# Retention attention and routed experts on one core: key-value states moved ahead, more load buffers, x stored for two chunks at a time

## The chip, the cores and the metric

The kernel runs on one core of one Trainium2 chip. A core has a matrix engine (TensorE, PE in the profile), VectorE (DVE), ScalarE (ACT), GpSimd (POOL) and SyncE (SP), which here only issues transfers, and 16 DMA engines[...]. The metric is device time in microseconds for one execution, lower is better; the number before is the median of three runs.

## What is computed

The first half is a retention layer on (8, 8, 576, 64) tensors (batch, heads, positions, head size), the second a mixture of eight experts with one expert for each token. Between them, x is the attention output with its heads side by side, 4608 tokens of 512 features.

```python
scores = scale * q @ k.T;  ret = scores * Dmat        # Dmat[i, j] = gamma[head] ** (i - j) for i >= j, else 0
x = (ret @ v), heads side by side                     # (8, 576, 512)
logits = x @ w_gate                                   # 8 experts
local_gate = sigmoid(x @ w_local)
e = argmax(logits) if s == 0 or local_gate < 0.5 else the expert of the token before
out[b, s] = softmax(logits)[e] * (relu(x[b, s] @ w1[e]) @ w2[e])
```

## The kernel before

The 4608 tokens are cut into NCH = 36 chunks of 128. A batch has 576 positions, so PER = 9 chunks hold two batches, and the middle one (MID, m = 4) belongs half to each. Retention is computed in chunks: inside a chunk by scores that are masked and multiplied with the values, and between chunks by a key-value state. The decay is folded into q (`decq`) and v (`deck`), so a state is a plain running sum of k times v in PSUM.

For chunk i there are four functions, and a loop at the end of the first part calls them skewed: in round i, `scores(i + 1)`, `outputs(i)`, `rows(i - 1)`, `logits(i - 2)`.

- `scores(i)` loads one tile `ld` (1 MB: q and k by feature, k and v by token; line 156, on SP's queue), scales q into `qT` (VectorE, line 165) and v into `vs` (GpSimd, line 169), multiplies k and q into two PSUM tiles `sps` (TensorE, line 176, eight matmuls) and masks them into `sT` (VectorE, line 180). For even i from 4 on it also issues, behind its own load, a 256 KB piece of the first expert's weights (line 162).
- `outputs(i)` multiplies `vs` with `sT` into the PSUM tile `ops` (line 202), adds the state of the chunk before times `qT` (line 211), adds this chunk's k times v to the PSUM tile `kv` (line 221) and copies that to one of two `states` tiles (ScalarE, line 224). Then ScalarE copies `ops` to `xT` (line 226).
- `rows(i)` computes gates and logits in parts from `xT` (line 234, ScalarE copies `parts`, line 237), turns `xT` into `x` with a VectorE transpose of 32 by 32 blocks (line 242) and stores x to DRAM (`xd`) in four transfers of 64 KB, issued by ScalarE (line 244).
- `logits(i)` adds the parts up (`lps`, line 254); after each of five groups of chunks the routing (`route`) goes on in small steps on VectorE, GpSimd and TensorE.

TensorE's order is the program order (a manual schedule); the other engines' order comes from the framework's scheduler. [...] Pools decide how many buffers a tile has: five for `ld`, four for `qT` and `vs`, three for `sT`, `xT` and `x`, one for `ops` and one for `kv`. A load of `ld` can't start before the last reader of its buffer is done. That reader is usually the state matmul, which reads the keys by token:

```python
nc.tensor.matmul(kv[r, c, :], lhsT=kn[k, h], rhs=vs[k, h], ...)      # kn = ld[:, 2]
```

Every transfer on SP's or ACT's queue counts on one of eight semaphores (DMAHW0 to DMAHW7 in the built program), which the framework deals out in turn. A transfer that reuses a semaphore waits until the transfer that last had it has landed; an engine that issues it stands still until then.

The second part comes when routing is done: the tokens of each expert are gathered from `xd` and taken through both weight matrices in blocks (lines 655 to 714). A first, small block with 256 tokens known early fills TensorE while the last routing steps run, from about 201 to 243 us.

Of the kernel before, what the change touches and what calls it, by code (L numbers as in the profile page):

```python
# [12 lines left out]
F32 = mybir.dt.float32  # L13
# [9 lines left out]
P = 128  # L23
# [3 lines left out]
DK, FK = D // P, F // P  # L27
HP = H // 2
NTOK = B * S
NCH = NTOK // P  # L30
PER = 2 * S // P
# [24 lines left out]
GW = E + 2  # L56
SQ = 32
NSQ = P // SQ
assert NSQ == DK


@with_exitstack
def kernel(
# [10 lines left out]
    nc = tc.nc  # L74

    def pool(stack, name, bufs, space=None):
        kw = {} if space is None else {"space": space}
        return stack.enter_context(tc.tile_pool(name=name, bufs=bufs, **kw))
# [6 lines left out]
    xd = dram.tile([NTOK, D], F32, name="xd")  # L85
# [32 lines left out]

    with ExitStack() as part:
        once = pool(part, "once", 1)  # L120
        raw = pool(part, "raw", 5)
        work = pool(part, "work", 3)
        ps_s = pool(part, "ps_s", 2, PSUM)
        ps_o = pool(part, "ps_o", 1, PSUM)
# [13 lines left out]
            out=mask, in_=mask, compare_op=Alu.is_ge, fill=0.0,  # L138
            base=0, pattern=[[1, P]], channel_multiplier=-1)
        states = [once.tile([P, HP, DH], F32, name=f"state{i}") for i in range(2)]  # L140
        chunks = [{} for _ in range(NCH)]
        to_lanes, routing = [], []
        kv = None

        def scores(i):
            m = i % PER
            g = chunks[i]
            ld = raw.tile([P, 4, D], F32, name="ld")
            if i == MID:
                nc.sync.dma_start(out=decq[:, m].rearrange("p c t -> p (c t)"), in_=dq[:, 1])  # L150
            elif 0 < i < PER:
                for c in range(HP):
                    nc.scalar.activation(decq[:, m, c], decq[:, 0, c], Act.Copy, scale=later_q[:, m, c:c + 1])
            cut = 4 if i == 0 else 1
            for k in range(0, 4, 4 // cut):
                loaded = nc.sync.dma_start(out=ld[:, k:k + 4 // cut].rearrange("p t x -> p (t x)"),
                                           in_=qkv[i][:, k * D:(k + 4 // cut) * D])
            if 4 <= i < 4 + 4 * FK and i % 2 == 0:

                k, t = divmod(i // 2 - 2, 2)  # L160
                with tc.issue_after(loaded.ins):
                    nc.sync.dma_start(out=(w2s[0][:, k] if t else w1s[0][:, k].rearrange("p k f -> p (k f)")),
                                      in_=(w2 if t else w1)[0][:, k * D:(k + 1) * D])
            qT = work.tile([P, HP, P], F32, name="qT", bufs=4)
            nc.vector.tensor_tensor(qT, ld[:, 0].rearrange("p (c s) -> p c s", c=HP), decq[:, m], op=Alu.mult)  # L165
            kT = ld[:, 1].rearrange("p (c s) -> p c s", c=HP)
            kn, vn = ld[:, 2], ld[:, 3]
            vs = work.tile([P, D], F32, name="vs", bufs=4)
            scaled = nc.gpsimd.tensor_tensor(  # L169
                vs.rearrange("p (h d) -> p h d", h=H), vn.rearrange("p (h d) -> p h d", h=H),  # L170
                deck[:, m, :].unsqueeze(2).to_broadcast([P, H, DH]), op=Alu.mult)
            sps = [ps_s.tile([P, HP, P], F32, name=f"sps{u}", tag="s") for u in range(2)]
            for c in range(HP):
                for u in range(2):
                    r = slice(u * DH, (u + 1) * DH)
                    nc.tensor.matmul(sps[u][:, c, :], lhsT=kT[r, c, :], rhs=qT[r, c, :],  # L176
                                     start=True, stop=True, skip_group_check=True)
            sT = work.tile([P, 2, HP, P], F32, name="sT")
            for u in range(2):
                nc.vector.tensor_tensor(  # L180
                    sT[:, u], sps[u],
                    (mask2 if m == MID else mask).unsqueeze(1).to_broadcast([P, HP, P]), op=Alu.mult)
            g.update(qT=qT, kn=kn, vs=vs, sT=sT)

            with tc.issue_after(scaled.ins):
                for write in to_lanes[:2]:
                    write()
            del to_lanes[:2]

        def outputs(i):  # L190
            nonlocal kv
            m = i % PER
            g = chunks[i]
            qT, kn, vs, sT = g["qT"], g["kn"], g["vs"], g["sT"]


            ops = ps_o.tile([P, 2, HP, P], F32, name="ops")
            for c in range(HP):
                for u in range(2):
                    r = slice((u ^ c & 1) * DH, ((u ^ c & 1) + 1) * DH)  # L200
                    h = 2 * c + u
                    nc.tensor.matmul(ops[r, c & 1, c // 2, :], lhsT=vs[:, h * DH:(h + 1) * DH], rhs=sT[:, u, c, :],  # L202
                                     start=(c < 2), stop=(m == 0), skip_group_check=True)
            if m > 0:

                n = HALF if m == MID else P
                for c in range(HP):
                    for u in range(2):
                        k = slice(u * DH, (u + 1) * DH)
                        r = slice((u ^ c & 1) * DH, ((u ^ c & 1) + 1) * DH)  # L210
                        nc.tensor.matmul(ops[r, c & 1, c // 2, 0:n], lhsT=states[(i + 1) % 2][k, c, :],
                                         rhs=qT[k, c, 0:n], start=False, stop=True, skip_group_check=True)
            if m != PER - 1:
                k = slice(HALF, P) if m == MID else slice(0, P)
                if m in (0, MID):
                    kv = ps_kv.tile([P, HP, DH], F32, name="kv")
                for c in range(HP):
                    for u in range(2):
                        r = slice(u * DH, (u + 1) * DH)
                        h = slice((2 * c + u) * DH, (2 * c + u + 1) * DH)  # L220
                        nc.tensor.matmul(kv[r, c, :], lhsT=kn[k, h], rhs=vs[k, h],
                                         start=(m in (0, MID) and c == 0), stop=True,
                                         skip_group_check=True)
                nc.scalar.copy(states[i % 2], kv)
            g["xT"] = xT = work.tile([P, HP, P], F32, name="xT")
            nc.scalar.copy(xT.rearrange("p (a b) t -> p b a t", b=2), ops[:, :, 0:HP // 2])  # L226

        def rows(i):
            nonlocal lt, lps
            xT = chunks[i]["xT"]  # L230

            gps = ps_g.tile([P, P], F32, name="gps")
            for c in range(DK):
                nc.tensor.matmul(gps[c * SQ:(c + 1) * SQ, :], lhsT=gates[:, c, :], rhs=xT[:, c, :],
                                 start=True, stop=True, skip_group_check=True)
            parts = work.tile([P, P], F32, name="parts")
            nc.scalar.copy(parts, gps)
            chunks[i]["parts"] = parts


            x = work.tile([P, NSQ, DK, SQ], F32, name="x")
            nc.vector.transpose(x.rearrange("p t c r -> p t c r"), xT.rearrange("p c (t s) -> p t c s", s=SQ))  # L242
            for a in range(NSQ):
                nc.scalar.dma_start(
                    out=xd[i * P:(i + 1) * P, a * P:(a + 1) * P].rearrange("(t s) d -> s t d", s=SQ),
                    in_=x[a * SQ:(a + 1) * SQ].rearrange("p t c r -> p t (c r)"))

        def logits(i):

# [141 lines left out]
        with tc.manual_schedule(engines={ET.PE}):  # L391
            scores(0)
            scores(1)
# [7 lines left out]
        def number(name, shape, pattern, base=0, channel=0, dtype=F32):  # L401
# [13 lines left out]
            out=before, in_=before, compare_op=Alu.is_gt, fill=0.0,  # L415
# [14 lines left out]
        low = table.tile([P, P], F32, name="low")  # L430
        nc.vector.memset(low, -1.0)
        last_e = low[:, 0:1]
        lt = lps = None

        add_parts = once.tile([P, GW], F32, name="add_parts")
        for c in range(DK):
# [3 lines left out]
        for M, at in ((P // 2, 0), (P // 4, 0), (P // 4, P // 2)):  # L440
            r = repeat[M, at] = table.tile([P, P], F32, name=f"repeat{M}_{at}")
# [13 lines left out]
        with tc.manual_schedule(engines={ET.PE}):  # L455
            for i in range(NCH + 2):
                if 1 < i + 1 < NCH:
                    scores(i + 1)
                if i < NCH:
                    outputs(i)  # L460
                if 0 <= i - 1 < NCH:
                    rows(i - 1)
                if 0 <= i - 2:
                    logits(i - 2)
                    for step in routing:
                        next(step, None)
                    if i - 2 in ends[:-1]:
                        k = ends.index(i - 2)
                        routing.append(route(starts[k], GROUPS[k], lt))
                if i == ends[SOON - 1] + 5:  # L470
                    base_soon = base
                if i == ends[SOON - 1] + 5 + -(-GROUPS[SOON - 1] // 2):
                    routing.append(load_soon())
# [368 lines left out]
```

## Time and profile before

| | |
|---|---|
| time, median of 3 | 786.47 us (783.32 to 786.67) |
| span of the profiled execution | 788.9 us |
| TensorE busy | 715.0 us (91%) |
| VectorE, ScalarE, GpSimd busy | 155.7, 157.3, 250.6 us |
| loads of `ld` | 35 of 1024 KB and 4 of 256 KB, 7.0 and 5.7 us from issue to landing (median) |
| stores of x | 144 of 64 KB, 5.1 us to landing |
| mean granted TensorE clock | 0.96 |

How to read it: a busy share is a mean over stages. The page's 40 slices show that VectorE works almost only in the first ten or eleven slices (to about 237 us), where attention and routing run. The DMA engines are mostly 0.6 to 0.9 busy for the first nine slices and then work in bursts. TensorE is busy in 0.9 or more of most slices after that. "Granted clock" is the share of full speed that the chip gave to TensorE in a stretch.

### The profile page before, as it was taken

The page shows a single profiled execution, that of the slowest core. Times are in us where ns is not written, and L with a number is a line of the kernel's source. Part 1 is how long each engine was busy: PE and PEld are TensorE (multiplying, and loading weights), DVE is VectorE, ACT ScalarE, POOL GpSimd, SP SyncE. Part 2 cuts the span into 40 slices and gives each one's busy share as a digit, 9 for nine tenths or more (in the row PEclk, how much of TensorE's full clock was granted, in tenths as well). Part 3 has the DMA queues.
Part 4 walks back from the last instruction along what each step waited for, and adds up shares of the span by engine and source line. Part 5 has one row for each costly group of instructions (what it writes and reads, how often), then busy time and mean ns, then how long its engine had stood idle before and what let it go on. Part 6 is the DMA issues. An engine that isn't in the chain of part 4 may idle for free. (4 is left out here: it accounts for less than half of the span.)

```text
span 788.9 us, 12435 instructions
## 1 busy us (share of the span) xinstructions
PE 715.0 (91%) x4932; PEld 475.6 (60%) x4932; DVE 155.7 (20%) x448; ACT 157.3 (20%) x396; POOL 250.6 (32%) x343
## 2 busy tenths in 40 slices
PE   3998789899769999998999999999999989989991
PEld 3767677677654546745764674576468457547740
DVE  5655656667770000000000000000000000000000
ACT  5312122122202102202211220211122021112110
POOL 4132525342757017006201700630170071025003
PEclk9998799998789999999999999999999999999997
DMA  8689788894007006104500710350071053013001
GB/s 338 212 289 315 243 287 278 278 301 121 25 0 247 17 30 254 49 2 147 200 1 30 275 47 2 109 232 1 23 268 66 2 183 141 1 57 117 2 16 62
DMA packets 46535, 103.90 MB, mean 132 GB/s; under 512 B 8264, under 2 KB 26828, under 8 KB 41936
## 3 DMA queue, kind: packets, MB, share of 16 engines
q0 software_dynamic: 17184, 50.36, 17.4%
q1 hardware_dynamic: 8064, 42.21, 15.3%
q10 hardware_dynamic: 21168, 9.83, 4.5%
q8 instruction: 64, 1.05, 0.6%
q14 instruction: 55, 0.45, 0.2%
HBM read 90.82 MB, written 24.12 MB: 146 GB/s over the span
## 5 line engine op out<-in xcount | busy, mean ns | idle before, releaser
L712 PE MATMUL hps<-xT,w1s 128*128 128x304 f32 (+4 forms) x1024 | 259.1, 415 | 0.1
L655 PE MATMUL yps<-w2s,hT 128*128 128x512 f32 x528 | 237.2, 597 | 0.3 <-issue 0.3
L712 PEld LDWEIGHTS hps<-xT,w1s 128*128 128x128 f32 x1024 | 195.6, 191 | 63.7 <-issue 13.7
L634 POOL DMA_INDIRECT out_dram<-ys,rows x49 | 48.7, 995 | 362.2 <-ACT ys L659 349.8
L655 PEld LDWEIGHTS yps<-w2s,hT 128*128 128x128 f32 x528 | 96.9, 191 | 106.3 <-issue 105.9
L714 ACT ACTIVATE hT<-hps 128x304 f32<-128x304 f32 (+4 forms) x128 | 53.5, 418 | 218.1 <-PE hps L712 218.1
L751 DVE MEMSET rows<- 128x1 int32 (+1 forms) x27 | 1.4, 60 | 443.2 <-DMA out_dram<-ys,rows 426.4
L169 POOL TENSOR_TENSOR vs<-ld,decs 128x512 f32<-128x512 f32 x36 | 47.1, 1309 | 100.3 <-DMA ld<-in_qkv_dram 80.6
L176 PE MATMUL sps<-qT,ld 64*128 64x128 f32 x576 | 54.6, 316 | 22.7 <-DVE sT L180 8.7
L623 POOL DMA_INDIRECT xg<-xd,slot x54 | 54.9, 1018 | 21.4 <-issue 12.2
L176 PEld LDWEIGHTS sps<-qT,ld 64*128 64x128 f32 x576 | 44.9, 213 | 27.7 <-DVE sT L180 12.9
L202 PE MATMUL ops<-sT,vs 128*64 128x128 f32 x576 | 46.3, 309 | 8.7 <-ACT xT L226 3.9
L659 ACT ACTIVATE ys<-yps,slot 128x512 f32<-128x512 f32 x31 | 21.3, 687 | 155.9 <-PE yps L655 155.9
L180 DVE TENSOR_TENSOR sT<-sps,mask 128x512 f32<-128x512 f32 x72 | 46.3, 677 | 11.5 <-PE sps L176 11.4
L202 PEld LDWEIGHTS ops<-sT,vs 128*64 128x64 f32 x576 | 36.5, 154 | 14.2 <-issue 9.8
L697 PEld LDWEIGHTS hps<-ident,xg 128*128 128x128 f32 (+3 forms) x164 | 19.9, 147 | 39.4 <-ACT xT L698 22.8
L226 ACT COPY xT<-ops 128x512 f32<-128x512 f32 x36 | 21.1, 587 | 110.2 <-DMA xd<-x 30.8
L697 PE MATMUL hps<-ident,xg 128*128 128x128 f32 (+3 forms) x164 | 25.2, 281 | 14.7 <-ACT xT L698 13.2
L165 DVE TENSOR_TENSOR qT<-ld,decq 128x512 f32<-128x512 f32 x36 | 27.2, 759 | 41.8 <-DMA ld<-in_qkv_dram 37.4
L682 PE MATMUL yps<-w2s,hT 128*32 128x128 f32 (+1 forms) x544 | 30.1, 306 | 0.0
L242 DVE STREAM_TRANSPOSE x<-xT 128x512 f32<-128x512 f32 x36 | 25.4, 706 | 17.7 <-ACT xT L226 16.9
L682 PEld LDWEIGHTS yps<-w2s,hT 128*32 128x32 f32 (+1 forms) x544 | 21.2, 118 | 5.2
(192 smaller groups left out, 406.0 us busy)
## 6 DMA issues: line engine op xcount, KB each, us to landing
ld<-in_qkv_dram SPq DMA_DIRECT2D x35, 1024.0 KB, 7.0
w1s<-in_w_dram POOLq DMA_DIRECT2D x32, 512.0 KB, 8.7
w2s<-in_w_dram POOLq DMA_DIRECT2D x32, 512.0 KB, 5.6
xd<-x ACTq DMA_DIRECT2D x144, 64.0 KB, 5.1
w1s<-in_w_dram SPq DMA_DIRECT2D x8, 256.0 KB, 5.6
w2s<-in_w_dram SPq DMA_DIRECT2D x8, 256.0 KB, 5.6
ld<-in_qkv_dram SPq DMA_DIRECT2D x4, 256.0 KB, 5.7
xg<-xd,slot POOLq DMA_INDIRECT x54, 6.2
```

The costliest lines, as they stand in the source:

```text
L165: nc.vector.tensor_tensor(qT, ld[:, 0].rearrange("p (c s) -> p c s", c=HP), decq[:, m], op=Alu.mult)
L169: scaled = nc.gpsimd.tensor_tensor(vs.rearrange("p (h d) -> p h d", h=H), vn.rearrange("p (h d) -> p h d", h=H), deck[:, m, :].unsqueeze(2 ...
L176: nc.tensor.matmul(sps[u][:, c, :], lhsT=kT[r, c, :], rhs=qT[r, c, :], start=True, stop=True, skip_group_check=True)
L180: nc.vector.tensor_tensor(sT[:, u], sps[u], (mask2 if m == MID else mask).unsqueeze(1).to_broadcast([P, HP, P]), op=Alu.mult)
L202: nc.tensor.matmul(ops[r, c & 1, c // 2, :], lhsT=vs[:, h * DH:(h + 1) * DH], rhs=sT[:, u, c, :], start=(c < 2), stop=(m == 0), skip_group ...
L623: nc.gpsimd.indirect_dma_start(out=xgs[j % 2][:, g, :], out_offset=None, in_=xd, in_offset=bass.IndirectOffsetOnAxis(ap=slot[:, g, 0:1], a ...
L634: nc.gpsimd.indirect_dma_start(out=next(views).rearrange("t (q d) -> (t q) d", q=n), out_offset=bass.IndirectOffsetOnAxis(ap=rows, axis=0) ...
L655: nc.tensor.matmul(yps, lhsT=hT[:, m, g * P:(g + 1) * P], rhs=w[:, m, :], start=(m == 0), stop=(m == FK - 1))
L682: nc.tensor.matmul(yps[q * M:(q + 1) * M, 0:D // n], lhsT=hT[:, m, first:first + M], rhs=w[:, m, q * D // n:(q + 1) * D // n], start=(m == ...
L697: nc.tensor.transpose(xps[:, c, 0:M], xg[0:M, g, c * P:(c + 1) * P], ident[0:M, 0:M])
L712: nc.tensor.matmul(hps[:, 0:T // n], lhsT=w[:, m, c, :], rhs=xT[:, c, cols], start=(c == 0), stop=(c == DK - 1))
L714: nc.scalar.activation(hT[:, m, cols], hps[:, 0:T // n], Act.Relu)
```

## The change

Three things are changed, all in the first part.

- The state work is taken out of `outputs` into a function `state(i)`, called right after `outputs(i - 1)`, so that it runs one round sooner; in round 0 `state(0)` and `state(1)` both run. It is meant to let go of the load buffer sooner, and to have the state ready well before its reader.
- `ld` gets seven buffers instead of five. The room comes from `sT` and `xT`, which go from three to two.
- x of two chunks lies in one tile (two such tiles, instead of three for one chunk each), and after the odd chunk four transfers of 128 KB store both, where there were eight of 64 KB. It halves the number of issues on ScalarE and of turns on the eight semaphores.

```diff
-        raw = pool(part, "raw", 5)
+        raw = pool(part, "raw", 7)
...
-            sT = work.tile([P, 2, HP, P], F32, name="sT")
+            sT = work.tile([P, 2, HP, P], F32, name="sT", bufs=2)
...
+            g["xT"] = xT = work.tile([P, HP, P], F32, name="xT", bufs=2)
+            nc.scalar.copy(xT.rearrange("p (a b) t -> p b a t", b=2), ops[:, :, 0:HP // 2])
+
+        def state(i):
+            nonlocal kv
+            m = i % PER
+            kn, vs = chunks[i]["kn"], chunks[i]["vs"]
             if m != PER - 1:
                 k = slice(HALF, P) if m == MID else slice(0, P)
...
                 nc.scalar.copy(states[i % 2], kv)
-            g["xT"] = xT = work.tile([P, HP, P], F32, name="xT")
-            nc.scalar.copy(xT.rearrange("p (a b) t -> p b a t", b=2), ops[:, :, 0:HP // 2])
...
-            x = work.tile([P, NSQ, DK, SQ], F32, name="x")
-            nc.vector.transpose(x.rearrange("p t c r -> p t c r"), xT.rearrange("p c (t s) -> p t c s", s=SQ))
-            for a in range(NSQ):
-                nc.scalar.dma_start(
-                    out=xd[i * P:(i + 1) * P, a * P:(a + 1) * P].rearrange("(t s) d -> s t d", s=SQ),
-                    in_=x[a * SQ:(a + 1) * SQ].rearrange("p t c r -> p t (c r)"))
+            if i % 2 == 0:
+                x = work.tile([P, 2, NSQ, DK, SQ], F32, name="x", bufs=2)
+            nc.vector.transpose(x[:, i % 2], xT.rearrange("p c (t s) -> p t c s", s=SQ))
+            if i % 2:
+                for a in range(NSQ):
+                    nc.scalar.dma_start(
+                        out=xd[(i - 1) * P:(i + 1) * P, a * P:(a + 1) * P].rearrange("(t s) d -> s t d", s=SQ),
+                        in_=x[a * SQ:(a + 1) * SQ].rearrange("p b t c r -> p (b t) (c r)"))
...
                     outputs(i)
+                    for k in (0, 1) if i == 0 else (i + 1,):
+                        if k < NCH:
+                            state(k)
```

More of the change, by code (lines that the diff above doesn't have):

```diff
@@ L58 @@
 NSQ = P // SQ
-assert NSQ == DK
+assert NSQ == DK and NCH % 2 == 0
 @with_exitstack
@@ L190, in outputs @@
         def outputs(i):
-            nonlocal kv
             m = i % PER
             g = chunks[i]
-            qT, kn, vs, sT = g["qT"], g["kn"], g["vs"], g["sT"]
+            qT, vs, sT = g["qT"], g["vs"], g["sT"]
             ops = ps_o.tile([P, 2, HP, P], F32, name="ops")
@@ L224, in outputs @@
                 nc.scalar.copy(states[i % 2], kv)
-            g["xT"] = xT = work.tile([P, HP, P], F32, name="xT")
-            nc.scalar.copy(xT.rearrange("p (a b) t -> p b a t", b=2), ops[:, :, 0:HP // 2])
         def rows(i):
-            nonlocal lt, lps
+            nonlocal x
             xT = chunks[i]["xT"]
@@ L432 @@
         last_e = low[:, 0:1]
-        lt = lps = None
+        lt = lps = x = None
         add_parts = once.tile([P, GW], F32, name="add_parts")
```

## The prediction

> **What bounds the kernel now.** I read the page first: TensorE busy for 91% of the span, the chain that ended last too short to help, VectorE busy in the first ten of the 40 slices only. So the kernel has two parts: attention with routing, to about 200 us, and the expert blocks, in which TensorE hardly stops. The change touches the first part alone, so I went on to the windows of ten microseconds (TensorE, its weight loads, VectorE, ScalarE, GpSimd, then granted clock, DMA share, GB/s).
>
> ```profile
> 10.00:20.00 10.00, 5.59 (x48) 4.55 (x48) 7.48 (x15) 3.77 (x12) 7.38 (x31) 1.00 1.01 407
> 20.00:30.00 10.00, 8.88 (x120) 7.36 (x120) 6.05 (x10) 3.96 (x12) 1.31 (x2) 1.00 0.39 116
> 60.00:70.00 10.00, 7.68 (x91) 6.34 (x90) 5.91 (x15) 1.16 (x4) 2.98 (x2) 0.71 0.99 332
> 80.00:90.00 10.00, 6.04 (x103) 5.02 (x104) 5.62 (x19) 2.06 (x6) 3.11 (x7) 0.91 0.86 278
> 90.00:100.00 10.00, 10.00 (x126) 8.17 (x129) 5.78 (x13) 1.79 (x4) 6.49 (x11) 0.58 0.60 186
> 0.00:180.00 180.00, 147.83 (x2317) 119.41 (x2317) 109.45 (x254) 45.59 (x126) 68.59 (x113) 0.93 0.84 282
> ```
>
> To see there: the DMA engines are full from 10 to 20, nearly idle from 20 to 30 (five load buffers are full, none is free), and 0.84 busy over 180 us: 151 us of work, 29 us of idling. A window with TensorE idle (60, 80) is followed by a low clock (0.71, 0.58). Next, the DMA queue's own waits (total, times, longest):
>
> ```profile
> SPq L156 <- DMA xd<-x: 52.0, 12, 8.3
> SPq L156 <- PE kv L221: 49.0, 14, 8.0
> SPq L162 <- DMA xd<-x: 22.4, 9, 3.8
> ```
>
> A load is held half the time by its buffer (the key-value matmul that reads `kn` last) and half by a store of x. The built instruction order shows why a load waits for a store: SP and ACT share eight DMA semaphores, DMAHW0 to 7, and a DMA waits until the one that last used its semaphore has landed. Stores take four turns for a chunk, a load one, a weight piece half of one. Then the timeline, once where loads are late and once where ScalarE is held:
>
> ```profile
> 62.48 0.69 DVE L165 TENSOR_TENSOR qT<-ld,decq 128x512 f32<-128x512 f32 x1 [3.85 <-DMA ld<-in_qkv_dram]
> ...
> 63.72 1.25 DVE L180 TENSOR_TENSOR sT<-sps,mask 128x512 f32<-128x512 f32 x2
> ...
> 64.43 0.79 PE L176 MATMUL sps<-qT,ld 64*128 64x128 f32 x2 [2.32 <-DVE sT L180]
> ```
>
> ```profile
> 106.61 4.19 ACTq L244 DMA_DIRECT2D xd<-x  x4
> 110.84 0.59 ACT L226 COPY xT<-ops 128x512 f32<-128x512 f32 x1 [5.73 <-DMA xd<-x]
> ...
> 111.57 1.03 PE L202 MATMUL ops<-sT,vs 128*64 128x128 f32 x11 [2.43 <-ACT xT L226]
> ```
>
> In the first, `qT` of a chunk two ahead stands before `sT` on VectorE, so a late load stops the scores. In the second, four stores wait for semaphores 4.19 us, `xT` stands behind them, and `ops` has one buffer, so TensorE stops. Last, the end of the stage: the last load's consumer and the last attention matmul.
>
> ```profile
> 181.84 1.04 POOL L169 TENSOR_TENSOR vs<-ld,decs 128x512 f32<-128x512 f32 x1 [3.00 <-DMA ld<-in_qkv_dram]
> ```
>
> ```profile
> 198.96 0.90 PE L254 MATMUL lps<-add_parts,parts 128*128 128x10 f32 x4
> ```
>
> So attention ends at 199.9 us, 18 us after its last load landed, and all that follows (589 us) hangs on that end.
>
> [...] low-clock windows follow the stalls at 60 and 80, and 16 scores matmuls took 2.67 us at 180 against 1.16 at full clock. [...] the windows above with share 0.99 to 1.01 are the ceiling that I use.
>
> **The change, part by part.** 1. State of chunk i+1 right behind `outputs(i)`. The matmuls are the same (484 in 27 to 200 us, 238 ns each); they run one chunk sooner, so `kn` is free one chunk, 4.0 us, earlier (state matmuls at 30.07 and 34.07 give the undisturbed period). It adds a wait of TensorE on `vs(i+1)`; behind it stand rows, logits and the next scores. `vs` takes 1.3 us after its load, and the scores of that chunk, which need the same load, stand a whole `outputs` (1.8 us) ahead: nothing. At the start `state(1)` waits for the copy of `state(0)` on ScalarE; both lie in the 5.3 us in which TensorE idles before 21.1 us anyway: gain below 1 us.
>
> 2. Seven load buffers instead of five. With part 1, load i+7 is free to go after outputs(i-1), instead of load i+5 after outputs(i): three chunks, 12 us, sooner, against a median landing of 6.9 us. Two loads more start before any buffer must come free and fill the hole from 20 to 30 (6.1 us of DMA time).
>
> 3. Two chunks' x in one set of four stores: 72 issues instead of 144. At a median of 0.446 us this takes 32 us off ScalarE, hidden by its idling (busy 37.5 of the 173 us from 27 to 200), so worth nothing by itself; in the worst case a double store takes double the issue time and nothing is saved. Bytes and 512-byte pieces stay, so DMA time stays. Semaphore turns fall from 5.5 to 3.5 a chunk. In the new order the stores before a load are two or three chunks older than its buffer's release. But 25 of the 72 stores wait for a load (29 of 144 before), and that load is four to five chunks ahead of TensorE: the store ahead of `xT(31)` waits for `ld(35)`, so `outputs(32)` can't start before the last load has landed.
>
> 4. `sT` and `xT` with two buffers: `sT(i)` waits for `outputs(i-2)` and `xT(i)` for rows i-2, both earlier on TensorE than what they need anyhow: nothing. `x` with two pair buffers: the transpose of chunk 2k waits for the stores of pair k-2, the last of which goes out some 8 us before. Landing takes 5.1 us (median), 9.2 at most; doubled in size I take 7. So 0, up to 2 us on VectorE for each of 16 pairs; behind it wait `qT` and `sT`.
>
> The sum. By `ld(35)`, 152.5 us of DMA work are done (0.84 x 180, and 1.5 at 0.87). In the new kernel I add the 2.2 us lost in the first ten, 4 us for a gap near 27 to 33, where `ld(9)` waits for the first, now later, pair of stores, and 3% of the remainder, 4 us: it lands at 163. Four chunks of 4.0 us and 1 us of gates and logits remain: attention ends at 180 instead of 199.9. TensorE would allow more: from 27 to 200 it idles 19.3 us and loses 0.09 x 173 = 15.6 us to the clock, so without stalls it would end at 165. DMA sets the end. Saving 20 us, time 786.5 - 20 = 766.5, say 767.
>
> **The rivals.** (a) Only a part comes: stores behind loads and the two x buffers still hold ScalarE and VectorE, and the DMA share rises from 0.86 (30 to 160 us) to 0.92 only. By 30 us 21.8 us of DMA work are done; 130.7 / 0.92 = 142, the last load at 172, end at 189: 776. For it: ScalarE waits 42.5 us for stores today and every fourth store or so still stands behind a load.
> (b) Better: no gap, the load stream at full share, `ld(35)` at 155, and three chunks after it: 168, 755. For it: share 1.0 with full queues from 10 to 20; against it: mixed windows at 0.98 moved only 300 GB/s.
> (c) No gain: the double stores land late (10.2 us, twice the median), each pair holds VectorE 2.2 us, 16 pairs 35 us; a fifth of it hidden, less the 20 saved: 794. Against it: VectorE waits only 0.7 us for stores today.
> (d) The clock falls more often in a denser stage. The trace speaks against it: from 242 on, with TensorE busy 517 of 547 us, the clock is 0.99. I give it nothing of its own.
>
> **How the numbers follow.** The forecast 0.46, (a) 0.30, (b) 0.12, (c) with its neighbours around no change 0.12. Faster by over 0.5% is the first three, 0.88; of (c), 0.04 within 0.5% and 0.08 slower. The range runs from just below (b), 754, to past (a), 783, and leaves out (c).
>
> **What would show it.** Right: attention's last `lps` near 180; DMA share from 20 to 30 near 0.8 and 0.93 or more from 40 to 160; SP's wait for `xd` under 20 us in place of 74, that for `kv` larger; half-clock windows fewer between 40 and 180; four chunks of TensorE after the last `vs`. Wrong: `xT` waiting on `xd` as long as before (a), or VectorE's transposes waiting on `xd` by tens of microseconds (c). If the share is high but GB/s stay at 285, the DMA ceiling was the mis-sized term.

## The result, and the profile after

| | before | after |
|---|---|---|
| time, median | 785.17 us (783.32 to 786.67, 4 runs) | 762.47 us (759.73 to 768.4, 4 runs) |
| ratio | | 0.9722, interval 0.9659 to 0.9786 |
| span of the profiled execution | 788.9 us | 766.8 us |
| end of attention (last `lps`) | 199.9 us | 181.8 us |
| the rest of the program | 589.0 us | 585.0 us |

A profile shows one execution, and some are longer than their median: 790.48 us for the kernel before, 768.4 for the change, 785.85 for e1 below (median 779.61). For the change, the median less the 585.0 us of the rest, and less the 1.6 us by which a time exceeds its span, puts a typical end near 176; that is an estimate.

The time is 4.5 us below the 767 that was forecast, and the end of attention in this profile 1.8 us behind the 180. Two terms on the way there were nevertheless wrong, in opposite directions, and the same views show it. First the windows, in the columns used before (TensorE, weight loads, VectorE, ScalarE, GpSimd, clock, DMA share, GB/s):

```profile
0.00:180.00 180.00, 155.52 (x2590) 127.05 (x2590) 127.28 (x294) 52.09 (x140) 66.02 (x124) 0.92 0.83 291
20.00:30.00 10.00, 8.87 (x116) 7.40 (x120) 5.50 (x10) 1.18 (x3) 1.47 (x3) 0.66 1.00 404
60.00:70.00 10.00, 7.58 (x85) 6.31 (x87) 7.21 (x19) 1.17 (x3) 1.04 (x1) 0.66 0.88 325
...
150.00:160.00 10.00, 10.00 (x160) 7.77 (x162) 6.60 (x17) 2.40 (x6) 5.13 (x7) 0.83 0.35 98
170.00:180.00 10.00, 10.00 (x185) 7.88 (x183) 7.83 (x27) 2.87 (x9) 2.21 (x9) 1.00 0.43 115
```

The hole from 20 to 30 is filled (share 1.00, where it was 0.39). The mean share to 180 has hardly changed (0.83, before 0.84). What has moved is where the DMA engines idle: now it is from 150 on, at 98 and 115 GB/s, with TensorE busy for all ten microseconds of each window. The transfers have run ahead. SP's and GpSimd's timelines give the last load's issue and the last `vs`, TensorE's the end:

```profile
144.25 0.33 SPq L156 DMA_DIRECT2D ld<-in_qkv_dram  x1
```

```profile
163.94 1.04 POOL L169 TENSOR_TENSOR vs<-ld,decs 128x512 f32<-128x512 f32 x1 [2.81 <-PE ops L201]
```

```profile
180.91 0.90 PE L260 MATMUL lps<-add_parts,parts 128*128 128x10 f32 x4
```

The last load is issued at 144 and lands 8.0 us later (the median of all loads is 8.2 us, 7.0 before), near 152 and 29 us before the end. The last `vs` no longer waits for its load, as it did before: it waits for the `outputs` matmul that reads the oldest of its four buffers. So the end of the stage hangs on TensorE, and TensorE is late because of these stalls (all with a wait in brackets from 27 to 180, in its timeline):

```profile
62.42 2.67 PE L176 MATMUL sps<-qT,ld 64*128 64x128 f32 x16 [4.52 <-DVE sT L180]
...
96.95 1.09 PE L201 MATMUL ops<-sT,vs 128*64 128x128 f32 x16 [2.81 <-ACT xT L213]
...
109.24 2.67 PE L176 MATMUL sps<-qT,ld 64*128 64x128 f32 x16 [1.92 <-DVE sT L180]
...
145.43 0.18 PE L331 MATMUL seen<-of_all,before 128*128 128x48 bf16 x1 [0.59 <-DVE of_all L327]
...
146.28 2.67 PE L176 MATMUL sps<-qT,ld 64*128 64x128 f32 x16 [0.53 <-DVE sT L180]
```

A stall can cost twice. The scores matmuls behind three of them take 2.67 us for 16, where those at 73.46, at a granted clock of 1.00, take 1.16; the clock records show stretches of 6.8 us at a granted clock of 0.50 from 61.3, 109.1 and 146.7. The stall of 2.81 us at 96.95 was followed by none (1.00 from 96.9 to 104). The stall at 62.42 comes from VectorE, in the timeline of all engines:

```profile
60.48 0.71 DVE L247 STREAM_TRANSPOSE x<-xT 128x512 f32<-128x512 f32 x1 [6.51 <-DMA xd<-x]
...
61.11 0.65 DVE L165 TENSOR_TENSOR qT<-ld,decq 128x512 f32<-128x512 f32 x1
...
61.68 1.28 DVE L180 TENSOR_TENSOR sT<-sps,mask 128x512 f32<-128x512 f32 x2
```

The transpose waits 6.51 us for a pair tile of `x`, and `qT` and `sT` stand behind it. The stall at 109.24 has the same cause (a 4.23 us wait). The one at 96.95 is the old one, `xT` behind stores on ScalarE (`ACTq` is its issuing side):

```profile
94.22 1.91 ACTq L250 DMA_DIRECT2D xd<-x  x2
...
96.22 0.59 ACT L213 COPY xT<-ops 128x512 f32<-128x512 f32 x1 [6.57 <-DVE sT L180]
```

The bracket names an earlier releaser; the two issues just ahead of it, 1.91 us, are what the copy stood behind last. The two short stalls, at 145.43 and 146.28, stand behind routing steps on VectorE. Last, the DMA queue's waits from 27 us on:

```profile
SPq L156 <- PE kv L227: 36.9, 10, 7.1
SPq L162 <- DMA xd<-x: 35.7, 8, 9.3
SPq L156 <- DMA xd<-x: 21.6, 4, 8.0
```

Loads and weight pieces still wait 57.3 us for stores (74.4 before), not under 20. What these waits cost is another matter, now that the queue is far ahead.

### The profile page after: what moved, and what is told of

It reads as the page before. It is cut to its first block, busy times and chain, and to the rows that moved or that the text cites. A ratio compares the mean times of both kernels' runs of the same rounds, so it can differ in the third digit from the quotient of the medians.

```text
span 766.8 us, 12329 instructions
## 1 busy us (share of the span) xinstructions
PE 705.4 (92%) x4932; PEld 469.5 (61%) x4932; DVE 160.5 (21%) x448; ACT 158.2 (21%) x396; POOL 243.6 (32%) x343
## 5 line engine op out<-in xcount | busy, mean ns | idle before, releaser
L664 PEld LDWEIGHTS yps<-w2s,hT 128*128 128x128 f32 x528 | 96.9, 191 | 105.7 <-issue 105.4
L169 POOL TENSOR_TENSOR vs<-ld,decs 128x512 f32<-128x512 f32 x36 | 38.7, 1077 | 95.7 <-PE ops L201 53.1
L176 PE MATMUL sps<-qT,ld 64*128 64x128 f32 x576 | 49.3, 308 | 19.6 <-DMA ld<-in_qkv_dram 7.0
L176 PEld LDWEIGHTS sps<-qT,ld 64*128 64x128 f32 x576 | 41.3, 207 | 22.3 <-issue 12.3
L180 DVE TENSOR_TENSOR sT<-sps,mask 128x512 f32<-128x512 f32 x72 | 45.9, 678 | 13.6 <-PE sps L176 13.6
L201 PE MATMUL ops<-sT,vs 128*64 128x128 f32 x576 | 44.3, 300 | 3.7 <-ACT xT L213 2.8
L201 PEld LDWEIGHTS ops<-sT,vs 128*64 128x64 f32 x576 | 34.6, 148 | 8.8 <-issue 3.9
L165 DVE TENSOR_TENSOR qT<-ld,decq 128x512 f32<-128x512 f32 x36 | 31.0, 865 | 8.8 <-PE ops L210 6.9
L247 DVE STREAM_TRANSPOSE x<-xT 128x512 f32<-128x512 f32 x36 | 25.3, 703 | 21.0 <-DMA xd<-x 13.6
```

Source lines behind the costliest of these rows:

```text
L169: scaled = nc.gpsimd.tensor_tensor(vs.rearrange("p (h d) -> p h d", h=H), vn.rearrange("p (h d) -> p h d", h=H), deck[:, m, :].unsqueeze(2 ...
L180: nc.vector.tensor_tensor(sT[:, u], sps[u], (mask2 if m == MID else mask).unsqueeze(1).to_broadcast([P, HP, P]), op=Alu.mult)
L664: nc.tensor.matmul(yps, lhsT=hT[:, m, g * P:(g + 1) * P], rhs=w[:, m, :], start=(m == 0), stop=(m == FK - 1))
```

## The experiments

Each ratio is to the kernel before, measured on the same chip; the rows come from several chips. "End" is the end of attention in the profiled execution. "Depth" below is how far ahead a load may run: the number of `ld` buffers, and whether `state` lets go of them a round early.

| kernel | `ld` buffers | state | stores of x | ratio (interval) | end, us |
|---|---|---|---|---|---|
| e1 | 7 | late | single | 0.9912 (0.9864 to 0.996) | 192.7 |
| e2 | 7 | early | single | 0.9957 (0.9929 to 0.9985) | 186.7 |
| e4 | 5 | late | pairs | 0.9884 (0.985 to 0.9919) | 183.6 |
| e11 | 6 | late | pairs | 0.9824 (0.9783 to 0.9865) | 177.5 |
| e5 | 6 | early | pairs | 0.9699 (0.9625 to 0.9774) | 174.7 |
| e3 | 7 | late | pairs | 0.9725 (0.9659 to 0.9792) | 173.8 |
| the change | 7 | early | pairs | 0.9722 (0.9659 to 0.9786) | 181.8 |
| e9 | 6 | late | pairs, three tiles | 0.9836 (0.9765 to 0.9907) | 180.8 |
| e6 | 6 | early | pairs, three tiles | 0.9692 (0.9605 to 0.9779) | 171.0 |
| e8 | 7 | late | pairs, all by GpSimd | 0.9815 (0.9735 to 0.9895) | 164.6 |
| e10 | 6 | late | pairs, three tiles, 14 of 18 by GpSimd | 0.9757 (0.9695 to 0.9818) | 177.7 |
| e12 | 7 | late | pairs, 14 of 18 by GpSimd | 0.9653 (0.9614 to 0.9692) | 166.6 |

### One part alone: more buffers (e1)

The kernel before, with the buffer numbers of the change:

```diff
-        raw = pool(part, "raw", 5)
+        raw = pool(part, "raw", 7)
...
-            sT = work.tile([P, 2, HP, P], F32, name="sT")
+            sT = work.tile([P, 2, HP, P], F32, name="sT", bufs=2)
...
-            g["xT"] = xT = work.tile([P, HP, P], F32, name="xT")
+            g["xT"] = xT = work.tile([P, HP, P], F32, name="xT", bufs=2)
```

> The kernel before with seven load buffers (sT and xT with two), state matmuls and single-chunk stores as before. Theory A (the depth of loading is what counted): most of the gain, 767 to 773 us, DMA share from 20 to 30 us near 0.9. Theory B (the semaphore turns of the stores were what counted): 778 to 784 us, SP's wait for stores of x stays near 74 us.

Measured: 0.9912, a third of the gain; the 779.61 us lie in the range of theory B. The end is no exact figure here, but the waits tell what kind of hold is left. TensorE's waits from 20 to 190 us:

```profile
PE ops L202 <- ACT xT L226: 15.5, 9, 4.1
```

The loads have room, and now `xT` stands behind stores on ScalarE nine times. The built instruction orders show why more buffers bring this about. The single stores wait for a load in 24 of 144 cases, and 17 of those 24 now wait for the load six chunks ahead, where 24 of 29 waited for one four chunks ahead in the kernel before. The semaphores are dealt in the order of issue, so a load issued further ahead makes a store wait for data that is further ahead.

### The change without its pair stores (e2)

```diff
...
-            if i % 2:
-                for a in range(NSQ):
-                    nc.scalar.dma_start(
-                        out=xd[(i - 1) * P:(i + 1) * P, a * P:(a + 1) * P].rearrange("(t s) d -> s t d", s=SQ),
...
+            for a in range(NSQ):
+                nc.scalar.dma_start(
+                    out=xd[i * P:(i + 1) * P, a * P:(a + 1) * P].rearrange("(t s) d -> s t d", s=SQ),
...
```

`x` is again a tile for one chunk, three of them; the early state and seven buffers stay.

> The changed kernel with x stored for each chunk by four transfers again (three x tiles), seven buffers and early states kept. Theory A: 762 to 768 us, since loading is as deep as in the changed kernel; a little faster than the changed kernel is possible, because the waits of VectorE for the two pair tiles (13.6 us there) go. Theory B: 772 to 780 us, with xT waiting on stores for 30 us or more again.

Measured: 0.9957, the smallest gain of all, and theory B again (779.39 us). TensorE's waits and the DMA queue's, both from 20 us on:

```profile
PE ops L201 <- ACT xT L213: 18.0, 12, 3.9
```

```profile
SPq L156 <- DMA xd<-x: 55.4, 15, 7.4
...
SPq L156 <- PE kv L227: 8.3, 4, 4.0
```

With all the depth the buffer hardly holds a load any more (8.3 us, 49.0 before), and almost nothing is gained. What the waits show instead is the exchange of semaphores between loads and stores: stores hold loads (55.4 us), and loads hold stores and with them `xT` (18.0 us of TensorE). Of the 25 stores that wait for a load, 12 wait for one seven chunks ahead. Depth is worth little while every chunk takes four turns for its stores: 0.4% here and 0.9% in e1, with intervals that overlap.

### The state late again (e3)

```diff
-                    for k in (0, 1) if i == 0 else (i + 1,):
-                        if k < NCH:
-                            state(k)
+                    state(i)
```

> The changed kernel with the state of chunk i behind outputs(i) again, so that a load buffer comes free one chunk later. Theory A, if depth still limits at seven buffers: 766 to 772 us. If seven buffers are more than enough (TensorE sets the end, the last load lands 30 us before it): 761 to 765 us, the same as the changed kernel.

Measured: 0.9725 against 0.9722. At seven buffers the early state cannot be told from none. The end came at 173.8 and so even earlier than the change's 181.8; the profiled executions differ by the stalls that they happen to have (one of 4.55 and one of 1.52 us on `xT` here). So a single end can scatter by some 8 us, and it is read below only together with the waits.

### One part alone: pair stores (e4)

The kernel before with `rows` of the change (pair tiles and four stores after the odd chunk), two buffers for `sT` and `xT`, five for `ld`.

> The kernel before with x stored for two chunks together (sT and xT with two buffers), five load buffers and late states. Theory A: 779 to 786 us, DMA share from 20 to 30 us stays near 0.4. Theory B: 768 to 775 us.

Measured: 0.9884 (774.10 us, in the range of theory B). The DMA queue's waits from 20 us on:

```profile
SPq L156 <- PE kv L221: 93.9, 23, 10.9
SPq L162 <- DMA xd<-x: 15.0, 6, 4.8
SPq L156 <- DMA xd<-x: 11.3, 3, 7.7
```

This is the mirror of e2: waits for stores fall from 74.4 to 26.3 us, and the buffer takes over, 93.9 us in place of 49.0. VectorE then waits 29.9 us for loads. Buffers alone bring 0.9%, pairs alone 1.2%, both together (e3) 2.75%. That is more than the sum of the two central values, but the intervals don't rule out a plain sum, and the order in which ScalarE copies `xT` and the state isn't the same in the three kernels. What is shown without the sum are the waits: each of the edits leaves the hold that the other removes.

### Six buffers, and three pair tiles (e5, e6)

```diff
-        raw = pool(part, "raw", 7)
+        raw = pool(part, "raw", 6)
```

and, in e6 only, with the room that this frees:

```diff
-                x = work.tile([P, 2, NSQ, DK, SQ], F32, name="x", bufs=2)
+                x = work.tile([P, 2, NSQ, DK, SQ], F32, name="x", bufs=3)
```

> The changed kernel with six load buffers instead of seven. If the depth of loading is used up (every buffer counts): 765 to 770 us. If TensorE sets the end and the rest is stalls: 760 to 765 us, the same as the changed kernel. Its main use is as the partner of the next run.

> Six load buffers and three pair tiles of x instead of two. If VectorE's waits for the pair tiles (6.5 and 4.2 us in the changed kernel, ahead of the two longest TensorE stalls) cost time: 3 to 10 us faster than the run with six buffers and two tiles, and VectorE's transposes wait under 2 us for stores. If the wait only moves to ScalarE's stores: within 2 us of it.

Measured: 0.9699 and 0.9692, both with intervals that overlap that of the change. The seventh buffer adds nothing that can be measured over the sixth when the state is early. The third pair tile does what it should inside the stage: VectorE's wait of `x` for stores, 13.6 us in four times in the change and 8.7 in e5, is gone in e6. Yet a stall at about the same place stays, for another reason. VectorE's and TensorE's timelines:

```profile
59.00 0.69 DVE L165 TENSOR_TENSOR qT<-ld,decq 128x512 f32<-128x512 f32 x1 [3.66 <-DMA ld<-in_qkv_dram]
```

```profile
60.34 2.67 PE L176 MATMUL sps<-qT,ld 64*128 64x128 f32 x16 [3.29 <-DVE sT L180]
...
105.08 1.09 PE L201 MATMUL ops<-sT,vs 128*64 128x128 f32 x16 [1.24 <-ACT xT L213]
```

Here the load is late. The queue's loads still wait 37.1 us for stores of x from 20 us on, 9.9 us the longest. ScalarE's `xT` still waits 20.4 us for stores, as in the change (20.1). The medians are 4.5 us apart, inside the 3 to 10 that were expected, but the ratios differ by only 0.0007 and the worth of the third tile is not resolved.

### A quarter of the loads' bytes away (e7)

The change, with v not loaded: keys are used in its place. This leaves out 9.4 MB (36 times 256 KB) of loads and alters the output, the routing and with it the expert part, so only the end of attention is read.

```diff
-            kn, vn = ld[:, 2], ld[:, 3]
+            kn, vn = ld[:, 2], ld[:, 2]
```

The loads fetch three quarters of a tile.

> The changed kernel without the load of v (the keys by token are used in its place), so 9.4 MB or a quarter of the load traffic is left out; the routing of tokens and the expert part change with it, so only the end of attention is read. If the DMA engines set the end (the step on record): attention ends near 155 us. If TensorE sets it: 175 to 182 us, as in the changed kernel (181.8), less only what stalls go.

Measured: `lps` at 155.4, end 156.3, 25.5 us sooner. The windows show why:

```profile
60.00:70.00 10.00, 10.00 (x196) 8.35 (x197) 9.17 (x23) 3.38 (x10) 2.81 (x4) 1.00 1.04 324
100.00:110.00 10.00, 10.00 (x190) 8.46 (x188) 9.26 (x29) 2.90 (x9) 8.68 (x17) 1.00 1.03 320
...
0.00:155.00 155.00, 144.23 (x2591) 118.36 (x2591) 128.42 (x295) 52.69 (x141) 67.12 (x125) 1.00 0.86 277
```

The time agrees with the theory that the DMA engines set the end, but the trace doesn't have its mechanism: the last load is issued at 123.6, some 33 us before the end. What is gone is every stall of TensorE between 27 and 180 and every half-clock stretch from 18.0, where its clock records begin, to 157.9. So 156 us is about what the stage takes when TensorE hardly waits, and the account of the change agrees with it: from 20 to 180 TensorE is idle for 160 - 148.1 = 11.9 us and its mean clock is 0.91, another 0.09 x 160 = 14.4 us; 181.8 - 26.3 = 155.5. In this stage, traffic costs time by way of stalls and the clock behind them, not by a last load that is late.

### The stores on another queue (e8, e12)

e3 with the pair stores issued by GpSimd, whose transfers count on eight other semaphores in the built program (DMASW0 to DMASW7):

```diff
-                    nc.scalar.dma_start(
+                    nc.gpsimd.dma_start(
```

> Seven buffers and pair tiles, states behind outputs(i), and the stores of x issued by GpSimd instead of ScalarE, so that ScalarE issues none and loads share no semaphore with stores. If ScalarE's standstill behind stores (20 us of waits for xT) and SP's waits for stores still cost time: 750 to 758 us. If GpSimd, with vs behind the stores, becomes the next holder: 762 to 775 us.

Measured: end of attention at 164.6, but the time is 763.96 us (0.9815), in the range of the second theory though not by its mechanism: the rest of the program takes 762.7 - 164.6 = 598.1 us, where it took 585.5 in e3. TensorE's timeline after attention, and GpSimd's:

```profile
173.25 5.83 PE L719 MATMUL hps<-xT,w1s 128*128 128x256 f32 x14 [3.12 <-ACT xT L705]
...
191.08 5.70 PE L108 MATMUL places<-w1s,lanes 128*128 128x220 bf16 x36 [11.99 <-POOL w1s L539]
```

```profile
165.54 1.75 POOL L487 TENSOR_SCALAR lanes<-numbers,lane_all 128x128 bf16<-128x128 f32 x3
167.25 2.39 POOL L250 DMA_DIRECT2D xd<-x  x4
```

The last stores stand between GpSimd's routing steps, and the first small block of the second part starts late and leaves TensorE idle for 12 us (5.39 in e3 ahead of the same matmul). So in e12 ScalarE issues the last four pairs:

```diff
-                    nc.gpsimd.dma_start(
+                    (nc.gpsimd if i < 28 else nc.scalar).dma_start(
```

> As the run in which GpSimd issues all stores (state late, seven buffers, two pair tiles), but ScalarE issues those of the last four pairs. Theory (depth brings the early end of attention, and only the last GpSimd stores lengthened what follows): last lps at 163 to 168, the rest 583 to 588 us after it, time 748 to 755, ratio 0.955 to 0.966. Rival (the last pairs on ScalarE bring the stalls back, or the 163.7 was scatter): last lps at 172 or later, time 758 or more.

Measured: 754.4 us (751.1 to 757.46), 0.9653, with the end at 166.6 and the rest 588.0. Its DMA queue from 20 to 160, and one window:

```profile
SPq L156 <- PE kv L227: 96.2, 24, 11.9
SPq L156 <- PE sps L176: 3.7, 3, 1.5
SPq L156 <- PE aps L301: 0.2, 1, 0.2
```

```profile
60.00:70.00 10.00, 10.00 (x197) 7.77 (x194) 7.90 (x17) 3.12 (x8) 6.07 (x10) 1.00 0.99 340
```

No load waits for a store any more, and from 27 to 165 TensorE waits 2.4 us in all. A wait of 96.2 us for the buffer, larger than the 49.0 that I read as half of the problem before, now costs next to nothing. My reading is that a queue which waits for the buffer has seven loads in flight or landed. This is the fastest kernel of the study by its median, and against the kernel before it is 3.5% faster; its interval ends at 0.9692 and overlaps those of e6 (755.39 us) and of the change, so it isn't shown to beat either.

### Is the early state worth anything? (e9, e10, e11)

e9 is e6 with the state late, e11 is e5 with the state late, each by the diff of e3. e10 is e9 with the first 14 pairs issued by GpSimd.

> State late, six load buffers, three pair tiles. Theory (the early state is worth nothing; depth and pair stores do it): ratio 0.962 to 0.975 and attention's last lps within 3 us of the same kernel with the state early (170.1), VectorE not waiting for a pair tile. Rival (the early state is what lets six buffers do the work of seven): lps at 175 or later, the queue's wait for the key-value matmul longer by 20 us or more, ratio above 0.978.

> As the run before, but GpSimd issues the stores of the first 14 pairs and ScalarE those of the last four. Theory (stores on ScalarE cause the stalls, and only the last GpSimd stores lengthened what follows): lps at 161 to 167 and the rest of the program back to 583 to 588 us after it, time 747 to 753, ratio 0.955 to 0.965. Rival (GpSimd's issues cost what follows whoever issues the last ones, since routing lanes on GpSimd run late): lps as early, the rest 595 us or more, time 759 to 764.

> As the run with six buffers, but with the state behind its own outputs. Theory (the early state counts as about one more chunk of depth, and at seven buffers it was only surplus): ratio 0.978 to 0.988, last lps at 177 to 184, the queue's wait for the key-value matmul 15 us or more above that of the kernel with six buffers and an early state. Rival (the early state is worth nothing, and the 180 of the late six-buffer kernel with three pair tiles is scatter): ratio 0.966 to 0.975, last lps at 172 to 176, wait for the key-value matmul within 10 us.

Measured: e9 0.9836 (e6: 0.9692), e11 0.9824 (e5: 0.9699). My theory for e9, that the early state is worth nothing, fell: its end is 9.7 us later than e6's and the wait for the buffer 27 us longer. e11, with the corrected theory, came out by it: the intervals of e11 and e5 don't overlap, though only just (0.9783 and 0.9774), and the two were measured on different chips; those of e9 and e6 overlap. The queue's wait for the key-value matmul from 20 to 185 us, first e5, then e11:

```profile
SPq L156 <- PE kv L227: 41.8, 12, 5.1
```

```profile
SPq L156 <- PE kv L227: 59.0, 17, 9.3
```

So depth counts, whichever way it is had: five late 0.9884, six late 0.9824, six early 0.9699, seven late 0.9725, seven early 0.9722. By these ratios it saturates at six buffers with an early state or seven without. That the state is also ready sooner for its reader plays no part that the waits show: TensorE's waits of 0.2 us or more in e11 have none for a state.

e10 gave 23.4 us against its kernel before, where 33 to 39 were expected. The rest of the program took 584.7 us, so the last stores were indeed what lengthened it in e8; but its end is 177.7, not 161 to 167. No load waits for a store there, and the wait for the buffer is 110.5 us: with the exchange of semaphores gone, six late buffers look too few, and the same kernel with seven (e12, which has two pair tiles where e10 has three) ends 11 us sooner.

## Why the forecast held, and which steps of it did not

**What bounds the stage.** Right as a reading: loads held half by the buffer, half by stores' semaphores. e2 and e4 take one hold away each and the other takes its place. What I did not see is how little either brings while the other stands.

**Part 1, the early state.** I counted it as 4 us of depth, one chunk, and that is borne out only where depth is short: at six buffers it is worth 1.2 to 1.4% by the central values (e5 and e6 against e11 and e9), at seven nothing that can be measured (e3). The gain below 1 us at the start is not told apart by any run.

**Part 2, seven buffers.** Three chunks sooner and the hole from 20 to 30 filled: both shown, the share there is 1.00. That three chunks are all wanted was wrong; two are enough (e3, e5).

**Part 3, pair stores.** Half the issues on ScalarE I costed at nothing by themselves, and the fall in turns as what matters. e2 against the change shows the worth of the pairs (the same depth brings 0.4% without them, 2.8% with them). It changes both at once; its waits speak for the turns (loads and weight pieces wait 76.3 us for stores in e2, 57.3 in the change; `xT` waits 37.6 and 20.1). I put the load on which a store waits at four to five chunks ahead of TensorE. The built order agrees: 14 of the 25 such stores wait for a load six or seven ahead of the later chunk that they store, and the `xT` behind them is two chunks on. Before, 24 of 29 waited for a load four ahead of the chunk stored. That is the price of depth; I had counted it, but gave it no time of its own.

**Part 4, the pair tiles.** I took 0, up to 2 us for each of 16 pairs. Measured: 13.6 us in four waits, the longest 6.51, so the mean is inside the bound, but they come in lumps, and a lump of 6.51 us or of 4.23 stopped TensorE for 4.52 and 1.92 us, while the wait of 1.27 us did not stop it. The landing that I took as 7 us has a median of 5.9, at most 13.3. The bound belonged on the longest wait, not on the mean.

**The sum.** "It lands at 163" and "four chunks of 4.0 us and 1 us remain" failed, both as times of the last load. It landed near 152 and the rest took 29 us: the queue ran further ahead, and so some of the stores that I had counted ahead of the last load came behind it (the windows after 150, share 0.35 to 0.43). "DMA sets the end" failed with them; the end is TensorE's, at a floor of 156 (I had put it at 165) with 26 us of stalls and lost clock. The two errors, 11 us too late and 12 us too short, cancelled, and so it is by luck that the 180 was nearly met. The four chunks after the last `vs` that I named as a sign did come (164.98 to 181.81, 16.8 us), but because `vs` has four buffers, not because of a load.

**The signs.** The share from 20 to 30 came as named, at 1.00 even above it; 0.93 or more from 40 to 160 did not (0.88 from 100 to 120, 0.63 from 140 to 160). The wait for stores (57.3 us, not under 20) and that for `kv` (36.9 us, smaller, not larger) were wrong in the change; the picture that I described is that of e12, where stores are off the semaphores. Half-clock stretches after the start fell from four to three between 40 and 180.

**The rivals.** (a), only a part comes, has the right waits (`xT` still waits 20.1 us for stores, 30.8 before) and the wrong sum, because TensorE was not bound to the last load. (c), double stores that land late, names a real cause of two stalls, but VectorE waited 13.6 us in all, not 35. (The 0.7 us that I set against it stand in the view before as a wait for a weight piece, not for a store.) (b) had the load stream nearly right (`ld(35)` at 155, and it landed near 152), and not its end at 168, for the reason that holds for the forecast: the end did not hang on the load. (d), the clock, stays at nothing: its low stretches became fewer, though those that are left cost 14.4 us.

What is not settled: how much of the change's 26 us is due to the pair tiles and how much to stores on ScalarE. An estimate from the stalls and half-clock stretches of this one trace gives 13 us to the two stalls behind pair tiles (4.52 + 1.92, and half of 2 x 6.8), 2.8 to the one behind stores on ScalarE, 4.5 to the two behind routing steps and 4.5 to the time from 20 to 27 us. But e6, which removes the first wait, got a stall behind a late load in its place, and e12, which removes the second from TensorE's path (`xT` still waits 9.9 us for stores), keeps 6.3 us of the first. Both have a smaller ratio than the change, neither by its interval.

## What to carry to other kernels

Loads and stores shared eight semaphores here, and prefetch depth and the number of stores were one problem: more buffers made a store wait for a load further ahead (six chunks instead of four in e1), and fewer stores left loads waiting for buffers (93.9 us in e4). So try both edits together before either is thrown away. Before a forecast takes "the last load lands, then so many chunks" for the end of a stage, subtract the compute engine's idle time and lost clock from the stage: if what is left is far below, as 155.5 us was below 181.8 in the change, stalls set the end, and the longest waits in each lane are worth more attention than their mean. And a transfer moved to another engine's queue should be moved back where that engine's own late work starts: the rest of the program took 598.1 us with all stores on GpSimd (e8) and 588.0 with the last four pairs on ScalarE (e12).

## What the runs showed of the hardware that was not expected

- A full DMA share is not one rate. At shares from 0.99 to 1.03 the windows moved 332 GB/s (before, 60 to 70), 404 (the change, 20 to 30) and 320 (e7, 100 to 110); I had taken 300 for mixed windows as a ceiling.
- Short stalls can be enough for the half clock, and their length alone doesn't decide. Behind waits of 1.92 us (109.24) and of 0.59 and 0.53 us within one microsecond (145.43 and 146.28) the change shows stretches of 6.8 us at a granted clock of 0.50, none behind 2.81 us (96.95). In e6 the clock stayed at 1.00 behind the wait of 1.24 us at 105.08 (100 to 120) and behind 1.23 us of idling between 130 and 140 (130 to 160). What decides is not shown by these runs.
- The same 128 KB stores leave fewer packet records when GpSimd issues them: with 56 of 72 moved (7.3 MB, e12 against e3), ScalarE's queue loses 15,232 packets and GpSimd's gains 2,688. e8, e10 and e12 therefore change the packets as well as the queue and the semaphores, and which of these ended the stalls was not tried.
